# The first layer's second half as seven block products, accumulated by its stores

## The chip, the cores and the metric

The kernel runs on one core of a Trainium2 chip. TensorE (PE) multiplies matrices into the PSUM memory, VectorE (DVE) and ScalarE (ACT) work element by element, GpSimd (POOL) helps out, and SyncE (SP) issues most transfers between the main memory (HBM) and the core's own memory (SBUF). The metric is device time in microseconds (us), the median of several runs. The profile is of one execution. Its times count from the first instruction.

## The reference, cut to what matters

Attention over 4 batches of 8 heads (576 tokens of 64 features, causal, mixed with a memory term by a gate per head) gives `x` of 2304 tokens by 512 features. Two feed-forward layers follow, each 512 to 2048 to 512 features, with different activations:

```python
def _moe_ref(x, w_in, w_out):
    h = x @ w_in
    g = np.where(h >= 1, h, np.where(h <= -1, 0.0, (h + 1) ** 2 / 4))
    return (g @ w_out).astype(np.float32)

def _moe2_ref(x, w_in, w_out):
    h = x @ w_in
    return (np.maximum(0.01 * h, h) @ w_out).astype(np.float32)
```

The layers' weights arrive as 64-bit floating point numbers. The kernel decodes them itself into 32-bit ones.

## The kernel before, in words

**Attention.** `attention_unit` does two heads of one batch, 16 units in all. A list scheduler (`Plan`, with room counts for the buffers, estimated costs and the priorities `PRIO`) writes out one fixed order for every engine before anything runs. Beside the units it schedules `weight_half`, the decoding of the first `EARLY` = 10 halves of weights: a load, two ACT instructions, five DVE instructions (lines 554, 567, 569, 571, 573) and a POOL subtraction (line 558). It also schedules `first_chunk`, which loads the first two token chunks of the layers.

**The layers.** The 2304 tokens are cut into 9 chunks of 256, in groups `(0,1) (2,3) (4,5) (6,7) (8)`: four pairs and a single chunk. There are four segments: layer 0 and layer 1, each in two halves of 1024 hidden features. A half is 8 slots `f` of 128 hidden features. Segment 1 is the second half of layer 0. A step computes the hidden values of one slot for a pair (12 matmuls of 512 columns, lines 798 to 800), or of two slots for the single chunk (24 matmuls of 256 columns). So a segment has 4 x 8 + 4 = 36 steps (`PER`). Every product is made as three matmuls of split operands (`three`: high times high, high times low, low times high), so each hidden value and each weight is needed as a high and a low part. `epilogue` applies the activation (layer 0: ACT lines 855 to 857, then a clamping on DVE, line 859) and makes the two parts (ACT line 865 or 873 the high, DVE line 867 or 875 the low).

**The second product.** About three steps later (`queue` and `pop` in `plan_steps`) PE multiplies those values with the output weights. Segments 0 and 1 do it plainly (`plain`: for each slot of a pair 4 tiles x 3 matmuls of 512 columns). Segments 2 and 3 have `SEVEN` set. There two slots and two column halves form a 2 x 2 block product, which `products` makes of 7 block products instead of 8, 21 matmuls of 256 columns for each chunk and pair of slots. This needs sums of blocks: of the hidden values (`minus` and `sums` in `epilogue`, DVE lines 880 to 885), of the weights (`keep_out` or `split_out`, with extra tiles `ex`), and of the results (`finish`: two ACT copies, line 944, and a third, line 961; DVE lines 948 to 957). The accumulators are the PSUM banks `Ya`, `Yb` and `Y3`. PE takes its tasks strictly by priority (`reach` 1 for PE), and the priority is the step.

**Where results go.** In layer 0 `finish_plain` copies a result into a buffer `lh` (two of them). In segment 0 it is stored to `y_d[0]`. In segment 1 the old sum is loaded into `pp` from `y_d[0]`, added on DVE (line 928) and stored to `y_d[1]`. `load_x` reads that as the input of layer 1. The layout there is features by tokens.

**Weights of later segments.** `weights` schedules, for segments 1 to 3, decoding ahead of time: 12 of 16 halves (`STAGED`: the 8 input halves, then 4 output halves) are decoded from step -29 in distances of 2.0 steps (`DECODE`), written to HBM (`w_d`, `ex_d`) and fetched when their place comes free (`FILL`). The other 4 are decoded directly at the segment's start (`DIRECT`). Transfers wait in order in SP's queue, so a waiting one holds back those behind it.

Of the kernel before, what the change touches and what calls it, by code (L numbers as in the profile page):

```python
# [19 lines left out]
NP = H // 2  # L20
# [8 lines left out]
SEVEN = (False, False, True, True)  # L29
NW, RAWB = 4, 3  # L30

PRIO = dict(load=-650.15, v=946.26, mem=425.05, k=42.8, q=46.21, phi=-70.12, f2=-1390.06, f3=-33.45, f4=-565.0, s0=-357.16,
            s1=-543.91, s2=-387.13, s3=-411.17, t0=49.18, t1=-152.47, t2=-67.16, t3=50.14, v0=-102.73, v1=231.04, v2=1621.08,
            v3=30.63, m=-186.73, d=-177.26, l=-633.13, xm=-415.81, xl=68.91, x=-762.94, b=67.46, w=(4.38, 21.56, 566.24),
            c=291.31)
EARLY, STAY = 10, 167.86
# [97 lines left out]
def attn_moe_moe_kernel(ctx, tc, q, k, v, m_prev, z_prev, beta, w1i, w1o, w2i, w2o, out):  # L134
# [24 lines left out]
    bt = const.tile([128, H], F32, name="bt")  # L159
    gate = const.tile([128, NP, 4], F32, name="gate")  # L160
    gates = const.tile([128, NP, 19], F32, name="gates")
# [15 lines left out]
    pick = const.tile([128, D], F32, name="pick")  # L177
# [57 lines left out]
    y_d = [{g[0]: dram.tile([128, 4, len(g), TC], F32, name=f"y_d{m}_{g[0]}") for g in GROUPS} for m in range(2)]  # L235
# [362 lines left out]
    steps = Plan(dict(x=2, ga=1, gb=1, gg=2, r=1, raw=RAWB - 1, xraw=2, h2=1, w32=NW, da=1, t=1, pp=1, s=1, lh=2, h=1, Ya=1, Yb=1, Y3=1,  # L598
# [16 lines left out]
    PER, AHEAD, DELAY, DIRECT_DELAY = 36, 2, 2, 2  # L615
# [105 lines left out]
    DECODE = [-29 + 2.0 * k for k in range(len(STAGED))]  # L721
    FILL = (-4, -3, -2, -1, -1, 0, 1, 2), (-1, 0, 2, 3)
    DIRECT = {4: 1, 5: 2.2, 6: 3.4, 7: 5}

    def weights(seg):

        base, kept, halves, todo = PER * seg, {}, [], []

        def stage(f, x, prio, after):
            parts = decode(seg, f, x, prio, after)  # L730
            if x == 0 or not SEVEN[seg]:
                kept[f, x] = [keep_half(seg, f, x, *parts, prio)[1]]
                return
            halves.append(parts)
            if f % 2:
                kept[f, x] = kept[f - 1, x] = keep_out(seg, f // 2, *zip(*halves), prio)
                halves.clear()

        def direct(f, prio, after):
            parts = decode(seg, f, 1, prio, after)  # L740
            if not SEVEN[seg]:
                split_half(seg, f, 1, *parts, prio)
                return
            halves.append(parts)
            if f % 2:
                split_out(seg, f // 2, *zip(*halves), prio)
                halves.clear()

        def fetch(room, src, prio, after):
            return steps.add("SP", SEND, prio, after, [room], lambda: nc.sync.dma_start(out=as_r(at(room)), in_=src), lag=6.0)  # L750

        def fill(f, x, prio, after):
            room, after = Room(f"o{f}" if x else f"in{f}"), [*after, *kept[f, x]]
            ready = fetch(room, w_d[seg][f, x], prio, after)
            if x == 0 or not SEVEN[seg]:
                half_room[seg, f, x], half_ready[seg, f, x] = room, ready
                return
            out_room.setdefault((seg, f // 2), []).append(room)
            out_ready.setdefault((seg, f // 2), []).append(ready)
            if f % 2:  # L760
                ex = Room(f"ex{f // 2}")
                out_room[seg, f // 2].append(ex)
                out_ready[seg, f // 2].append(fetch(ex, ex_d[seg][f // 2], prio, after))

        for (f, x), when in zip(STAGED, DECODE):
            todo.append((base + when - AHEAD, lambda after, f=f, x=x, when=when: stage(f, x, base + when + DELAY, after)))
            at_step = FILL[x][f]
            todo.append((base + at_step, lambda after, f=f, x=x, a=at_step: fill(f, x, base + a, after)))
        for f, when in DIRECT.items():
            todo.append((base + when - AHEAD, lambda after, f=f, when=when: direct(f, base + when + DIRECT_DELAY, after)))  # L770
        return todo

    def load_x(seg, group, prio, mm):

        room, ready, n = Room("x"), [], group[0]
        for j, c in enumerate(group):
            raw = Room("xraw")

            def load(c=c, raw=raw):
                xf = staging(at(raw))  # L780
                if SEGS[seg][0] == 0:
                    load_chunk(c, xf)
                else:
                    nc.sync.dma_start(out=xf, in_=y_d[1][n][:, :, c - n])
# [126 lines left out]
    def finish_plain(seg, group, banks, lhs, after, step):  # L911
        half, pair, n, add = SEGS[seg][1], len(group) == 2, group[0], steps.add
        for i, lh in enumerate(lhs):
# [9 lines left out]
            ts = [t]  # L923
            if half:
                pp = Room("pp")
                before = add("SP", SEND, step - 2, [stored_y[seg - 1, n, i]], [pp], lambda pp=pp, place=place: nc.sync.dma_start(
                    out=at(pp).rearrange("p k j t -> p (k j) t"), in_=place(y_d[0])), lag=4.6)
                ts = [add("DVE", dve(512), step, [t, before], [lh, pp], lambda k=k, lh=lh, pp=pp: vec.tensor_tensor(
                    at(lh)[k], at(lh)[k], at(pp)[:, k], ALU.add), lag=SLACK) for k in range(2)]
            t = add("SP", SEND, step + 0.2, ts, [lh], lambda lh=lh, place=place: nc.sync.dma_start(  # L930
                out=place(y_d[half]), in_=at(lh)[2]), lag=4.0)
            stored_y[seg, n, i] = t
            if half:
                for c in group:
                    stored_y.setdefault((seg + 1, c), []).append(t)

    def finish(seg, group, j, banks, y3, lhs, after, step):

        half, pair, c = SEGS[seg][1], len(group) == 2, group[j]
        s, lh, add, tt = Room("s"), lhs[j], steps.add, vec.tensor_tensor  # L940

# [4 lines left out]
        def sums_a():  # L946
            (s0, s1), (lo, hi) = at(s), at(lh)[0:2]
# [6 lines left out]
        def sums_b():  # L954
            (s0, s1), (lo, hi) = at(s), at(lh)[0:2]
            tt(lo[:, 1], s1[:, 0], s1[:, 1], ALU.add)
            tt(lo[:, 0], s1[:, 0], lo[:, 0], ALU.subtract)

        if j == 0:
            for i in range(1 + pair):  # L960
                add("ACT", from_psum(256), step - 2, after, [y3, lhs[i]], lambda i=i: act.activation(
                    at(lhs[i])[0][:, 0], at(y3)[:, i], AF.Copy))
# [3 lines left out]
        ts, goal = [t, t], op_d[c]  # L966
        if half:
            pp, goal = Room("pp"), out[TC * c:TC * c + TC].rearrange("(i p) m -> p i m", i=2)
            before = add("SP", SEND, step - 1, [stored_y[seg - 1, c]], [pp], lambda: load_kept(pp, c), lag=4.0)
            ts = [add("DVE", dve(512), step, [t, before], [lh, pp], lambda i=i: vec.tensor_tensor(  # L970
                at(lh)[i], at(lh)[i], at(pp)[:, i], ALU.add), lag=SLACK) for i in range(2)]
        stored_y[seg, c] = add("SP", SEND, step + 0.2, ts, [lh], lambda: nc.sync.dma_start(
            out=goal, in_=at(lh)[2].rearrange("p (i a) t -> p i (a t)", i=2)), lag=4.0)
# [153 lines left out]
    def take(name, *shape, dt=F32):  # L1127
# [5 lines left out]
                 gg=[[take(f"g{t}{i}", 7, 256, dt=F32R) for t in "hl"] for i in range(2)], r=[take("r", 512)],  # L1133
# [42 lines left out]
```

## Time and profile before

| | us |
|---|---|
| median of 3 runs | 992.94 (992.47 to 993.09) |
| the profiled execution, device time | 992.16 |
| its span from first to last instruction | 990.4 |
| its mean granted TensorE clock | 0.999 of full speed |

The page of the profile gives each engine's busy time and share of the span, then the span in 40 slices, the queues, the chain of work that ended last (followed back from the last instruction), and the costliest groups of instructions. The granted clock is at its upper level, 2.4 GHz, in every slice. A row of a timeline names start, duration, engine, line, operation and output and input. Matmuls overlap, so their durations (0.39 us for 512 columns) are longer than the distance from one start to the next. Attention takes the first 210 us. Then come the segments, with the first steps of segments 1, 2 and 3 at 399, 596 and 787 us.

### The profile page before, as it was taken

The numbers are of one execution on the slowest core, as the hardware profiler recorded it, in microseconds if no ns is written. First come the engines' busy times: TensorE is split into PE (matmuls) and PEld (weight loads), VectorE is DVE, ScalarE is ACT, GpSimd is POOL, SyncE is SP. The second block draws the span as 40 slices with busy tenths as digits, with TensorE's granted clock in tenths as the row PEclk, the third lists the DMA queues.
The fourth block names the chain that finished last, engine by engine and source line by source line (L and its number), as shares of the span: only waits on it lengthen the run. The fifth ranks groups of instructions, "written<-read, shape, count | busy, mean of one in ns | idle before, by whom it ended". The sixth has DMA issues, their size and how long they took to land.

```text
span 990.4 us, 19703 instructions
## 1 busy us (share of the span) xinstructions
PE 975.8 (99%) x7794; PEld 861.4 (87%) x7794; DVE 719.1 (73%) x1569; ACT 597.3 (60%) x1052; POOL 46.4 (5%) x74
## 2 busy tenths in 40 slices
PE   7999999999999999999999999999999999999997
PEld 6888899988888889988888899999999999999997
DVE  7999977759766553486675746997977988755746
ACT  7899888866756465566564654555544554443433
POOL 1332221100000000000000000000000000000000
PEclk9999999999999999999999999999999999999999
DMA  9666743112535442935462669353425790302112
GB/s 199 170 149 152 164 119 98 48 63 90 192 125 173 149 146 80 339 112 157 154 203 70 220 222 355 114 191 133 144 108 181 276 339 13 128 19 89 58 50 85
DMA packets 128556, 145.47 MB, mean 147 GB/s; under 512 B 67792, under 2 KB 103376, under 8 KB 128464
## 3 DMA queue, kind: packets, MB, share of 16 engines
q1 hardware_dynamic: 126976, 143.66, 45.5%
q8 instruction: 61, 1.00, 0.4%
q10 hardware_dynamic: 1488, 0.56, 0.2%
q14 instruction: 31, 0.25, 0.1%
HBM read 98.58 MB, written 45.61 MB: 146 GB/s over the span
## 4 chain that ended last, share of the span: by engine, by line
PE 82%; DVE 9%; ACT 5%; issue 2%; DMA 1%; SPq 0%; DVEq 0%; ACTq 0%
PE h L798 13%; PE h L799 13%; PE h L800 13%; PE Y L799 13%; PE Y L800 13%; PE Y L798 13%; DVE e L403 3%; ACT e L408 3%; PE W L293 2%; DVE ks L348 1%; PE W L438 1%; ACT pt L416 1%; DVE da L567 1%; DVE xm L491 1%; PE W L384 0%
## 5 line engine op out<-in xcount | busy, mean ns | idle before, releaser
L798 PE MATMUL h<-xh,i 128*128 128x512 f32 (+1 forms) x320 | 118.3, 370 | 0.0
L799 PE MATMUL h<-xl,i 128*128 128x512 f32 (+1 forms) x320 | 118.1, 369 | 0.0
L799 PE MATMUL Y<-gl,o 128*128 128x512 f32 (+1 forms) x320 | 117.8, 368 | 0.0
L798 PE MATMUL Y<-gh,o 128*128 128x512 f32 (+1 forms) x320 | 117.7, 368 | 0.0
L800 PE MATMUL h<-xh,i 128*128 128x512 f32 (+1 forms) x320 | 117.7, 368 | 0.0
L800 PE MATMUL Y<-gh,o 128*128 128x512 f32 (+1 forms) x320 | 117.7, 368 | 0.0
L798 PE MATMUL h<-ffn_x,i 128*128 128x512 f32 (+1 forms) x312 | 115.2, 369 | 0.0
L799 PE MATMUL h<-ffn_x,i 128*128 128x512 f32 (+1 forms) x312 | 115.0, 369 | 0.0
L800 PE MATMUL h<-ffn_x,i 128*128 128x512 f32 (+1 forms) x312 | 114.6, 367 | 0.0
L855 ACT ACTIVATE r<-h 128x512 f32<-128x512 f32 x70 | 41.9, 599 | 117.3 <-PE h L800 117.2
L408 ACT ACTIVATE e<-e,mx 128x384 f32<-128x384 f32 (+4 forms) x144 | 71.8, 576 | 16.8 <-DVE mx L403 16.7
L800 PE MATMUL Y<-o,gl 128*128 128x256 f32 x288 | 81.5, 283 | 0.0
L799 PE MATMUL Y<-o,gh 128*128 128x256 f32 x288 | 81.5, 283 | 0.0
L798 PE MATMUL Y<-o,gh 128*128 128x256 f32 x288 | 81.2, 282 | 0.0
L859 DVE SCALAR_TENSOR_TENSOR ga<-ga,r 128x512 f32<-128x512 f32 (+1 forms) x40 | 25.6, 639 | 70.9 <-ACT r L857 70.8
L800 PEld LDWEIGHTS h<-xh,i 128*128 128x128 f32 x320 | 60.3, 189 | 10.3
L865 ACT ACTIVATE gh<-gb 128x512 fp32r<-128x512 f32 (+1 forms) x72 | 53.1, 738 | 26.7 <-DVE gb L885 25.6
L798 PEld LDWEIGHTS Y<-gh,o 128*128 128x128 f32 x320 | 60.3, 189 | 10.1
L800 PEld LDWEIGHTS Y<-gh,o 128*128 128x128 f32 x320 | 60.3, 188 | 10.0
L799 PEld LDWEIGHTS Y<-gl,o 128*128 128x128 f32 x320 | 60.3, 189 | 9.9
L798 PEld LDWEIGHTS h<-xh,i 128*128 128x128 f32 x320 | 60.5, 189 | 9.5 <-ACT gb L852 0.2
L799 PEld LDWEIGHTS h<-xl,i 128*128 128x128 f32 x320 | 60.5, 189 | 8.8
(177 smaller groups left out, 2373.0 us busy)
## 6 DMA issues: line engine op xcount, KB each, us to landing
w_d<-raw SPq DMA_DIRECT2D x36, 512.0 KB, 3.0
raw<-in_moe_w_in_dram SPq DMA_DIRECT2D x32, 512.0 KB, 4.0
raw<-in_moe_w_out_dram SPq DMA_DIRECT2D x32, 512.0 KB, 4.9
i<-w_d SPq DMA_DIRECT2D x24, 512.0 KB, 5.7
y_d<-lh SPq DMA_DIRECT2D x18, 512.0 KB, 4.0
raw<-y_d SPq DMA_DIRECT2D x18, 512.0 KB, 5.9
raw<-x_d SPq DMA_DIRECT2D x12, 512.0 KB, 5.2
o<-w_d SPq DMA_DIRECT2D x12, 512.0 KB, 8.0
```

The lines of the kernel that those rows point to most:

```text
L293: pe.transpose(t[:, c:c + 128], x, ident)
L348: k3 = add("DVE", dve(S), "k", [k2], [t, ks], lambda t=t: vec.tensor_tensor(at(ks)[:, 1], at(t)[:, 0:S], as_r(at(ks)[:, 0]), ALU.subtract))
L403: vec.tensor_tensor_reduce(out=out, in0=src, in1=mk, op0=ALU.add, op1=ALU.min, scale=1.0, scalar=3e38, accum_out=at(st)[1][:, col:col + 1])
L408: lambda x=x, w=w, col=col: act.activation(at(x)[:, 0:w], at(x)[:, 0:w], AF.Exp, bias=at(st)[1][:, col:col + 1], scale=-1.0))
L416: return add("ACT", from_psum(n), key, [t1], [t, room], lambda: act.activation(at(room)[:, 0:n], at(t)[:, 0:n], AF.Copy))
L438: pe.matmul(o[r:r + 64, a:a + W1], at(pt)[:, c + r:c + r + 64], x[:, j, h], start=(j == 0), stop=(j == i))
L798: pe.matmul(o, wh, xh, start=first, stop=False)
L799: pe.matmul(o, wh, xl, start=False, stop=False)
L800: pe.matmul(o, wl, xh, start=False, stop=last)
L855: t1 = add("ACT", from_psum(512), prio, [mm], [hp, r], lambda: act.activation(at(r), at(hp), AF.Relu, bias=0.5, scale=0.5))
L859: new.append(add("DVE", dve(512 if pair else 256), prio, [t, t1], [g[k], r], lambda k=k: vec.scalar_tensor_tensor(out=fresh(k), in0=fresh( ...
L865: h = add("ACT", from_sbuf(width * (b - a)), prio + late, after, [x, gg], lambda: act.activation(view(at(gg)[0])[:, a + c:b + c], view(at( ...
```

## The change

Segment 1 is now a `SEVEN` segment too. Its results come out of `finish`. For the pairs, a POOL transfer adds them onto what segment 0 stored in `y_d` (`accum_op`), so `pp`, the load of the old sum and its addition on DVE go for pairs. The product of the single chunk comes out with tokens on the partitions. `turn_single` turns it with 8 transposes on PE, adds the old sum on DVE and stores it on SP. `y_d` is one array per group instead of two. There are two buffers `r` (half of the activation's square) instead of one. Segment 2's staged decoding has a schedule of its own (`DECODE2`): two halves at steps -64 and -58, so in segment 0, and ten from -30 in distances of 2.3. For segments 1 and 3 the distance is 2.2. The direct decoding of segments 1 and 2 starts 0.5 to 1 step earlier and has a shorter delay (0.5 for 2). Attention decodes 11 halves instead of 10, and all priorities of its plan have other values. Four small tiles move into attention's pool.

```diff
-SEVEN = (False, False, True, True)
+SEVEN = (False, True, True, True)
...
-PRIO = dict(load=-650.15, v=946.26, mem=425.05, k=42.8, q=46.21, phi=-70.12, f2=-1390.06, f3=-33.45, f4=-565.0, s0=-357.16,
...
-            c=291.31)
-EARLY, STAY = 10, 167.86
+PRIO = dict(load=-577.73, v=756.58, mem=328.18, k=39.63, q=46.87, phi=-28.29, f2=-1253.86, f3=-158.15, f4=-1035.0,
...
+            w=(4.77, 24.07, 535.6), c=189.81)
+EARLY, STAY = 11, 157.01
...
-    y_d = [{g[0]: dram.tile([128, 4, len(g), TC], F32, name=f"y_d{m}_{g[0]}") for g in GROUPS} for m in range(2)]
+    y_d = {g[0]: dram.tile([128, 4, len(g), TC], F32, name=f"y_d{g[0]}") for g in GROUPS}
...
-    DECODE = [-29 + 2.0 * k for k in range(len(STAGED))]
+    DECODE = [-30 + 2.2 * k for k in range(len(STAGED))]
+    DECODE2 = [-64 + 6 * k for k in range(2)] + [-30 + 2.3 * k for k in range(10)]
...
-    DIRECT = {4: 1, 5: 2.2, 6: 3.4, 7: 5}
+    DIRECT, DIRECT3 = ({4: 0, 5: 1.5, 6: 3, 7: 4.5}, 0.5), ({4: 1, 5: 2.2, 6: 3.4, 7: 5}, 2)
...
-            if half:
-                pp = Room("pp")
-                before = add("SP", SEND, step - 2, [stored_y[seg - 1, n, i]], [pp], lambda pp=pp, place=place: nc.sync.dma_start(
-                    out=at(pp).rearrange("p k j t -> p (k j) t"), in_=place(y_d[0])), lag=4.6)
-                ts = [add("DVE", dve(512), step, [t, before], [lh, pp], lambda k=k, lh=lh, pp=pp: vec.tensor_tensor(
-                    at(lh)[k], at(lh)[k], at(pp)[:, k], ALU.add), lag=SLACK) for k in range(2)]
...
+        if layer == 0 and not pair:
+            return turn_single(lh, t, banks, step)
+
+        if layer == 0:
+            def add_up():
+                pool.dma_start(out=y_d[n].rearrange("p (b j) i t -> p j b (i t)", j=2)[:, j],
+                               in_=at(lh)[2].rearrange("p (i a) t -> p i (a t)", i=2), accum_op=ALU.add)
+
+            t = add("POOL", 1200, step + 0.2, [t, *(stored_y[0, n, i] for i in range(2))], [lh], add_up, lag=6.0)
+            for x in group:
+                stored_y.setdefault((2, x), []).append(t)
+            return
...
+    def turn_single(lh, t, used, step):
+
+        n, banks, res, pp, add = NCH - 1, Room(used.kind), Room("lh"), Room("pp"), steps.add
+
+        def turn():
+            for i in range(2):
+                x = at(lh)[i].rearrange("p a t -> p (a t)")
+                for et in range(4):
+                    pe.transpose(at(banks)[et // 2][:, et % 2, 128 * i:128 * i + 128], x[:, 128 * et:128 * et + 128], ident)
...
+        before = add("SP", SEND, step - 1, [stored_y[0, n, 0]], [pp], lambda: nc.sync.dma_start(
+            out=at(pp).rearrange("p i a t -> p (i a) t"), in_=whole(y_d)), lag=5.0)
+        t = add("PE", 900, step + 1.2, [t], [lh, banks], turn)
+        ts = [add("DVE", dve(512), step - 1, [t, before], [banks, res, pp], lambda i=i: vec.tensor_tensor(
+            at(res)[i], at(banks)[i], at(pp)[:, i], ALU.add)) for i in range(2)]
+        t = add("SP", SEND, step + 2, ts, [res], lambda: nc.sync.dma_start(out=whole(y_d), in_=at(res)[2]), lag=4.0)
+        stored_y.setdefault((2, n), []).append(t)
...
-                 gg=[[take(f"g{t}{i}", 7, 256, dt=F32R) for t in "hl"] for i in range(2)], r=[take("r", 512)],
+                 gg=[[take(f"g{t}{i}", 7, 256, dt=F32R) for t in "hl"] for i in range(2)], r=[take("r0", 512), take("r1", 512)],
```

## Rows read from the trace of the kernel before

**Rows 1.** The page: busy time of the engines; the last chain by engine.

```profile
PE 975.8 (99%) x7794; PEld 861.4 (87%) x7794; DVE 719.1 (73%) x1569; ACT 597.3 (60%) x1052; POOL 46.4 (5%) x74
...
PE 82%; DVE 9%; ACT 5%; issue 2%; DMA 1%; SPq 0%; DVEq 0%; ACTq 0%
```

**Rows 2.** Timeline of PE (start, us, instruction): first matmuls of groups.

```profile
210.27 0.48 PE L798 MATMUL h<-ffn_x,i 128*128 128x512 f32 x1
...
442.98 0.39 PE L798 MATMUL h<-ffn_x,i 128*128 128x512 f32 x1
...
486.50 0.39 PE L798 MATMUL h<-xh,i 128*128 128x512 f32 x1
...
639.67 0.40 PE L798 MATMUL h<-xh,i 128*128 128x512 f32 x1
...
681.75 0.40 PE L798 MATMUL h<-ffn_x,i 128*128 128x512 f32 x1
```

**Rows 3.** Timeline of DVE in attention, line 355, once a unit ([idle before]).

```profile
46.69 0.75 DVE L355 SCALAR_TENSOR_TENSOR qs<-W,qs 128x576 fp32r<-128x576 f32 x1
...
96.21 0.75 DVE L355 SCALAR_TENSOR_TENSOR qs<-W,qs 128x576 fp32r<-128x576 f32 x1
...
157.66 0.76 DVE L355 SCALAR_TENSOR_TENSOR qs<-W,qs 128x576 fp32r<-128x576 f32 x1 [2.93 <-ACT qs L353]
...
169.61 0.76 DVE L355 SCALAR_TENSOR_TENSOR qs<-W,qs 128x576 fp32r<-128x576 f32 x1 [2.94 <-ACT qs L353]
```

**Rows 4.** Timeline of PE in attention: a run of transposes and what follows.

```profile
164.42 3.08 PE L293 MATMUL W<-ident,e 128*128 128x128 f32 x25
167.33 0.60 PE L342 MATMUL W<-ident,q 128*128 128x128 f32 x4
```

**Rows 5.** Groups of ACT, 640 to 682 us (busy us, mean ns | idle).

```profile
L944 ACT ACTIVATE s<-Y 128x512 f32<-128x512 f32 x4 | 2.2, 597 | 0.0
```

**Rows 6.** Groups of DVE, 640 to 682 us.

```profile
L867 DVE TENSOR_TENSOR gl<-gb,gh 128x512 fp32r<-128x512 f32 (+1 forms) x10 | 8.2, 819 | 0.3 <-ACT gh L865 0.3
...
L957 DVE TENSOR_TENSOR lh<-s,lh 128x256 f32<-128x256 f32 x2 | 0.8, 418 | 0.0
```

**Rows 7.** Windows: length, busy PE, PEld, DVE, ACT, POOL, clock, DMA share, GB/s.

```profile
147.00:159.00 12.00, 11.95 (x221) 10.84 (x218) 8.75 (x32) 10.40 (x19) 1.91 (x4) 1.00 0.47 112
...
443.00:487.00 44.00, 44.00 (x196) 36.44 (x195) 28.81 (x46) 26.57 (x48) 0.00 (x0) 1.00 0.52 168
...
640.00:682.00 42.00, 42.00 (x266) 38.07 (x265) 37.78 (x73) 23.05 (x38) 0.00 (x0) 1.00 0.46 154
...
766.00:787.00 21.00, 21.00 (x177) 20.98 (x176) 19.90 (x45) 11.87 (x27) 0.00 (x0) 1.00 0.66 222
```

**Rows 8.** Groups of DVE, 443 to 487 us: half of the clampings.

```profile
L859 DVE SCALAR_TENSOR_TENSOR gb<-gb,r 128x512 f32<-128x512 f32 x4 | 2.8, 693 | 9.1 <-ACT r L857 9.1
```

**Rows 9.** Groups of DVE, 0 to 209 us: decoding's five instructions.

```profile
L567 DVE SCALAR_TENSOR_TENSOR da<-w,da 128x512 int32<-128x512 int32 x10 | 8.9, 886 | 0.2
...
L573 DVE TENSOR_TENSOR w<-da,dr 128x512 f32<-128x512 f32 x10 | 7.6, 755 | 0.1
L571 DVE SCALAR_TENSOR_TENSOR dr<-raw,dr 128x512 f32<-128x512 uint32 x10 | 6.9, 686 | 0.1
L569 DVE TENSOR_SCALAR dr<-da 128x512 int32<-128x512 int32 x10 | 6.4, 643 | 0.1
...
L554 DVE TENSOR_SCALAR da<-raw 128x512 int32<-128x512 int32 x10 | 4.9, 490 | 0.1
```

**Rows 10.** Transfers of the whole run: KB each, median us to landing.

```profile
y_d<-lh SPq DMA_DIRECT2D x18, 512.0 KB, 4.0
...
pp<-y_d SPq DMA_DIRECT2D x9, 512.0 KB, 4.9
```

**Rows 11.** Timelines of POOL and DVE around 108 us.

```profile
108.06 1.28 POOL L533 TENSOR_TENSOR xr<-xr,xm 128x512 f32<-128x512 f32 x1 [8.69 <-DVE xr L503]
...
108.51 1.38 DVE L567 SCALAR_TENSOR_TENSOR da<-w,da 128x512 int32<-128x512 int32 x1
```

## What I expect, and why

> **What bounds the kernel now.** I read the page's first and fourth parts first: TensorE (PE) is busy for 99% of the span and carries 82% of the chain that ended last, VectorE (DVE) 9% [rows 1]. Busy is modelled for a pipelined engine, so I went on to the waits and the timeline of PE. From 210 us, where the two layers begin, the view of waits names none for PE, and the starts of its matmuls follow each other without a hole, across the ends of chunk groups too: a pair group in the plain form, 192 matmuls of 512 columns, takes 486.50 − 442.98 = 43.52 us [rows 2], 0.2267 us each. So the layers (780 of 990 us) are bound by PE's matmuls, and other work there costs time only where it makes PE wait. The first 210 us, attention, are different. Up to some 120 us DVE starts each instruction as the last ends and a unit takes longer; later DVE sits idle ahead of the same instruction in each unit and PE sets the pace [rows 3].
>
> **The part that the change is about.** A segment has 36 steps: 8 for each of four pairs of chunks and 4 for the single chunk. Segment 1 (the first layer's second half) makes its second product in full, segments 2 and 3 make it of seven block products. Both forms are in the trace, so the gain can be read. A pair takes 43.52 us in the plain form and 681.75 − 639.67 = 42.08 us in the seven form [rows 2]: 1.44 us a pair, 5.76 us for four. (By columns alone it would be an eighth of the product's 21.8 us, 2.7 us; but 42.08 − 96 x 0.2267 = 20.3 us for 168 matmuls of 256 columns is 0.121 us each, and two of them take 0.015 us more than one of 512. That eats almost half.) The single chunk's product has 256 columns in both forms, 8 features x 4 column tiles x 3 = 96 matmuls before and 4 x 7 x 3 = 84 after: 12 x 0.12 = 1.44 us less. Together **−7.20 us** on PE.
>
> **New work on PE.** In the seven form the single chunk's result has tokens on the partitions, while the intermediate array wants features there; `turn_single` adds 8 transposes for it. 25 such transposes took 167.33 − 164.42 = 2.91 us, 0.116 each [rows 4]: **+0.93 us**. They stand in PE's fixed order between two batches of segment 2's first group, and all of segment 2 is queued behind them. They wait for the finish of the single chunk: three ScalarE copies of at most 0.6 us [rows 5], then seven DVE sums of 0.42 [rows 6], 4.7 us. In between PE has the first product of a step (12 x 0.227 = 2.7 us) and a batch of 24 block matmuls (2.9 us), 5.6 us, so they are covered by 0.9 us and the wait is put at 0; with no cover it would be 4.7 us, once. Two DVE additions (0.69 each) must then clear the bank within the next 2.7 us.
>
> **DVE in segment 1** is the cover for all of this, and I cost it from two sides. From the seven side: the second group of segment 2 keeps DVE busy for 37.78 of 42.00 us [rows 7]. The same group in the first layer has 8 clampings of the activation more, 8 x 0.69 = 5.5 [rows 8]; decoding for segment 2 goes from a half every 2.0 steps to one every 2.3, half a weight half less per group, 3.46/2 = 1.7 us [rows 9]. 37.8 + 5.5 − 1.7 = 41.6 us of 42.1. From the plain side: 28.81 us now [rows 7], plus 16 sums of 0.42 (6.7), plus low parts of 8.2 [rows 6] and 4 of 0.69 in place of 8 of 0.69 (5.4), plus the finish, 14 sums of 0.42 in place of 4 additions of 0.69 (3.1), minus 1.7: 42.3, an upper end, since durations of neighbours overlap a little. So DVE is 99 to 101% full. That is tight, but in segment 2's single-chunk window it is busy for 19.90 of 21.00 us while PE misses nothing [rows 7], and PE's second product runs three steps of 5.4 us behind the activations, so that a light group makes up for a full one. The two halves moved to segment 0 and the second `r` buffer lighten it further. Bounds for PE's wait: 0, and (42.3 − 42.1) x 4 = 0.8 us, plus as much at the two ends of the segment. I take **+0.5 us**. In segment 0 the combining and the two halves cost nothing: a plain group leaves DVE idle for 15 of 44 us [rows 7], which covers them; without it each half would cost its 3.5 us.
>
> **The accumulating stores.** Eight stores on GpSimd's queue replace 8 loads of the old sum, 16 DVE additions (counted above) and 8 stores on SP's queue. GpSimd's 46 us of work [rows 1] lie in attention, so nothing is queued behind their wait for the sums. No row shows such a store. The nearest are the plain store and the load that it replaces, 4.0 and 4.9 us to landing [rows 10], 8.9 us together. What waits for it: the `lh` buffer, at the tightest place (last pair to single chunk) four steps of 5.4 us less some 5 us for the sums, so it may take about 16 us; and the next layer's load, over 20 steps later. Cost between 0 and, at twice 8.9 us, 2 us once; I take 0, as 8.9 is nearer. For DVE the nearest row is a GpSimd addition of 1.28 us, beside which a DVE instruction on 512 columns took 1.38 us [rows 11] where 0.69 is usual [rows 8]: 0 to 0.7 us of DVE a store. I take 0, since a store's data don't pass through GpSimd. The Trainium skill, "SBUF — State Buffer", section Who interferes with whom, states that a DVE instruction with two SBUF inputs contends with GpSimd instructions that read SBUF, not with those that only write it; [rows 11] agree with the first half, and no run here shows the second. By that rule an issue that only writes descriptors would cost these sums nothing; one that reads would cost up to 8 x 0.7 = 5.6 us of DVE.
>
> SP's queue loses 16 transfers in segment 1 and gets 6 stores and 2 loads of combined weights; the loads and stores of two halves go to segment 0. No wait of PE in the layers follows a transfer now, and segment 2, which has the same loads, shows none at its start: 0, and if one fill came late, its 5 to 9 us less the steps ahead of it.
>
> **Attention** decodes an eleventh half: five DVE instructions, 0.49 + 0.89 + 0.64 + 0.69 + 0.76 = 3.46 us [rows 9]. Segment 0 then has one less, and no wait to win there. Where DVE is full a unit takes (96.21 − 46.69)/4 = 12.38 us, elsewhere 169.61 − 157.66 = 11.95 [rows 3]. After 120 us the half would cost 0, since DVE is busy only 8.75 of 12 us there [rows 7]; all on the path it costs 3.5. About one half is decoded per unit, so the likeliest is one more full unit: **+0.4 us**. All other priorities of this stage change too. The trace prices that only from both sides: eight full units lose 8 x 0.43 = 3.4 us, which a better order could win back, and I allow as much for a worse one. I take 0 and keep both ends.
>
> **Sum.** The profiled execution took 992.16 us (span 990.4): 992.16 − 7.20 + 0.93 + 0.5 + 0.4 = 986.8. It lies 0.8 below the median of the runs, 992.94, so the forecast for the median is **987.5 us**, 0.55% less; with the small bounds 985.3 to 989.5.
>
> **Rivals.** (a) Attention gains from its new order, 984.1 to 985.3. For it: 3.4 us lie there; against: no row says that the new order finds them. Chance 0.11. (b) Part of the gain is lost to DVE in segment 1 or to waits at its ends: 42.6 to 43.4 us of DVE a group make 0.5 to 1.3 us of wait each, 2 to 5 us: 989.5 to 993. For it: 99 to 101%; against: 95% without a hole in segment 2. 0.13. (c) Attention loses 2 to 5 us, the half wholly on the path and a worse order: 989.5 to 992.5. 0.07. (d) Slower: DVE becomes the bound all through segment 1. Place: its four pair groups, 400 to 575 us. Price: 42.3 us and two stores that each hold DVE for a whole 1.28 us: 44.9, 2.8 over, 11.2 us for four, 998. It decides from 43.5 us a group, where 4 x 1.4 takes back the gain of 5.5; from 44 the kernel is slower. Against it: the issue of a store must hold DVE as long as a computing instruction of GpSimd. 0.07. (e) The seven form gains nothing in the first layer, where the weights stand still and the activations move, the other way about than in segment 2: 994.7. Against it: loads of 128x128 and 256 columns in both. 0.02.
>
> **How the numbers follow.** The forecast (985.3 to 989.5) has 0.60. A measurement of this kernel tells about 0.2%, 2 us, from no change: faster is under 990.95, slower over 994.9. Faster: 0.60, (a), half of (b) and two thirds of (c), 0.82. Same: the rest of (b) and (c), (e), and a little of (d), 0.12. Slower: 0.06. The range takes in the forecast, the near half of (a), and (b) and (c) up to 990.9: 984.7 to 990.9.
>
> **What would show it.** Right: first matmuls of the pair groups of segment 1 42.1 us apart; eight transposes shortly after segment 1 with no hole ahead of them; DVE at 40 to 42 us a group there; segment 2 as now; the first matmul of the layers, now at 210.3 us [rows 2], at 210.7. Wrong: holes in PE's starts in segment 1 that DVE or ScalarE ends (b, d); DVE instructions stretched beside GpSimd's issues (d); accumulating stores that land after more than 16 us and a wait for `lh`; a first matmul that moves by over 2 us (a, c).

## The result, and the profile after

The changed kernel takes 1000.69 us (999.08 to 1001.19, 6 runs) against 992.71 before: 1.0077 times as long, interval 1.0064 to 1.0090. I had forecast 987.5. It is slower by 0.8%, outside my range and on the other side. This is the page of its profile, busy time and the last chain by engine:

```profile
span 999.0 us, 20513 instructions
...
PE 974.7 (98%) x8078; PEld 872.4 (87%) x8078; DVE 787.4 (79%) x1733; ACT 617.0 (62%) x1083; POOL 55.5 (6%) x83
...
PE 76%; DVE 17%; DMA 3%; issue 2%; ACT 1%; SPq 1%; DVEq 0%; ACTq 0%
```

Against [rows 1], PE is busy for no longer, but carries 76% of the chain instead of 82%. DVE has gone from 9 to 17%, and DMA from 1 to 3%. The timeline of PE tells where. These are first matmuls, to be read beside [rows 2]:

```profile
218.47 0.48 PE L800 MATMUL h<-ffn_x,i 128*128 128x512 f32 x1
...
450.63 0.40 PE L800 MATMUL h<-ffn_x,i 128*128 128x512 f32 x1
...
492.71 0.40 PE L800 MATMUL h<-xh,i 128*128 128x512 f32 x1
...
792.02 0.40 PE L800 MATMUL h<-xh,i 128*128 128x512 f32 x1
...
838.41 0.40 PE L800 MATMUL h<-ffn_x,i 128*128 128x512 f32 x1
```

The layers begin at 218.47 instead of 210.27 us: **attention lost 8.2 us**. A pair group of segment 1 takes 492.71 − 450.63 = 42.08 us, exactly the seven form's time. But segment 3's first group, which the change to the product doesn't touch, takes 838.41 − 792.02 = 46.39 us, and 829.98 − 787.42 = 42.56 by these rows of the kernel before:

```profile
787.42 0.50 PE L798 MATMUL h<-xh,i 128*128 128x512 f32 x1
...
829.98 0.40 PE L798 MATMUL h<-ffn_x,i 128*128 128x512 f32 x1
```

From the first matmul to the end of the span the layers take 999.0 − 218.5 = 780.5 us, and 780.1 before: **their gain is used up inside them**. PE's waits from 218 us on, which the kernel before didn't have (us in total, times, longest):

```profile
PE h L800 <- ACT ga L854: 2.1, 1, 2.1
PE Y L997 <- DVE lh L954: 1.2, 1, 1.2
PE h L800 <- ACT gb L858: 1.0, 1, 1.0
PE h L800 <- ACT ga L858: 0.3, 1, 0.3
```

The first is at 808 us, 16 us into segment 3. The matmuls behind it are slow too, so it costs 3.8 us. The others are the wait ahead of the transposes (621 us), the end of segment 1 (599 us) and the end of its last pair (561 us). Together that is some 6.5 us (6.8 by the distances between the matmuls' starts), what was to be gained on balance (7.20 − 0.93 = 6.3).

**Attention.** Line 355 on DVE, once a unit, beside [rows 3]:

```profile
48.74 0.75 DVE L355 SCALAR_TENSOR_TENSOR qs<-W,qs 128x576 fp32r<-128x576 f32 x1
...
100.73 0.75 DVE L355 SCALAR_TENSOR_TENSOR qs<-W,qs 128x576 fp32r<-128x576 f32 x1
...
164.34 0.76 DVE L355 SCALAR_TENSOR_TENSOR qs<-W,qs 128x576 fp32r<-128x576 f32 x1 [2.68 <-ACT qs L353]
...
176.76 0.76 DVE L355 SCALAR_TENSOR_TENSOR qs<-W,qs 128x576 fp32r<-128x576 f32 x1 [2.68 <-ACT qs L353]
```

A unit takes (100.73 − 48.74)/4 = 13.00 us where DVE is full (12.38 before) and 12.42 where it isn't (11.95 before). Both stretches are slower, so two things may be at work. The first shows in the decoding's instructions, 0 to 217 us, beside [rows 9]:

```profile
L567 DVE SCALAR_TENSOR_TENSOR da<-w,da 128x512 int32<-128x512 int32 x11 | 10.7, 976 | 0.3
L573 DVE TENSOR_TENSOR w<-da,dr 128x512 f32<-128x512 f32 x11 | 8.9, 813 | 0.1
...
L569 DVE TENSOR_SCALAR dr<-da 128x512 int32<-128x512 int32 x11 | 8.6, 780 | 0.1
L571 DVE SCALAR_TENSOR_TENSOR dr<-raw,dr 128x512 f32<-128x512 uint32 x11 | 8.2, 749 | 0.1
L554 DVE TENSOR_SCALAR da<-raw 128x512 int32<-128x512 int32 x11 | 6.0, 549 | 0.1
```

The same instructions take longer on average, because more of them take some 0.7 us more. POOL is running whenever one does:

```profile
76.33 1.29 POOL L558 TENSOR_TENSOR o<-w,o 128x512 fp32r<-128x512 f32 x1 [0.18 <-ACT o L562]
...
102.28 1.29 POOL L558 TENSOR_TENSOR o<-w,o 128x512 fp32r<-128x512 f32 x1
```

```profile
76.93 1.24 DVE L567 SCALAR_TENSOR_TENSOR da<-w,da 128x512 int32<-128x512 int32 x1
...
102.72 1.39 DVE L567 SCALAR_TENSOR_TENSOR da<-w,da 128x512 int32<-128x512 int32 x1
```

POOL's instruction ends at 77.62 and at 103.57. The DVE instruction ends 0.55 us after each, so it held still until POOL was nearly done. Summed over the stretched instructions (each one's time over the tenth percentile of its shape) this is 11.5 us after and 6.5 before. Beside line 533, the local sum, it is 6.2 and 5.6. Beside line 558, the decoding's own subtraction, it is 5.3 and 0.9. In the old order POOL's subtraction mostly runs while DVE works on scores out of PSUM (line 403), and none of those is stretched. In the new order the next half's decode instructions stand there.

### The profile page after: what moved, and what is told of

The parts are those of the page before. It is cut to its first block, busy times and chain, and to the rows that moved or that the text cites. A ratio compares the mean times of both kernels' runs of the same rounds, so it can differ in the third digit from the quotient of the medians.

```text
span 999.0 us, 20513 instructions
## 1 busy us (share of the span) xinstructions
PE 974.7 (98%) x8078; PEld 872.4 (87%) x8078; DVE 787.4 (79%) x1733; ACT 617.0 (62%) x1083; POOL 55.5 (6%) x83
## 4 chain that ended last, share of the span: by engine, by line
PE 76%; DVE 17%; DMA 3%; issue 2%; ACT 1%; SPq 1%; DVEq 0%; ACTq 0%
PE h L800 12%; PE h L801 12%; PE h L802 12%; PE Y L802 11%; PE Y L801 11%; PE Y L800 11%; DVE e L403 5%; DMA raw<-in_moe_w_out_dram 2%; PE W L438 2%; DVE xm L491 1%; DVE xr L503 1%; PE W L293 1%; DMA o<-w_d 1%; DVE dr L569 1%; PE W L434 1%
## 5 line engine op out<-in xcount | busy, mean ns | idle before, releaser
L867 ACT ACTIVATE gh<-gb 128x512 fp32r<-128x512 f32 (+1 forms) x108 | 79.8, 739 | 41.7 <-DVE gb L887 33.6
L801 PE MATMUL Y<-gl,o 128*128 128x256 f32 (+1 forms) x288 | 95.1, 330 | 0.0
L802 PE MATMUL Y<-gh,o 128*128 128x256 f32 (+1 forms) x288 | 95.1, 330 | 0.0
L800 PE MATMUL Y<-gh,o 128*128 128x256 f32 (+1 forms) x288 | 94.9, 330 | 0.0
L869 DVE TENSOR_TENSOR gl<-gb,gh 128x512 fp32r<-128x512 f32 (+1 forms) x108 | 88.4, 820 | 7.0 <-ACT gh L867 7.0
L802 PE MATMUL Y<-o,gl 128*128 128x256 f32 x304 | 86.0, 283 | 0.0
L801 PE MATMUL Y<-o,gh 128*128 128x256 f32 x304 | 86.0, 283 | 0.0
L800 PE MATMUL Y<-o,gh 128*128 128x256 f32 x304 | 85.7, 282 | 0.0
L403 DVE CUSTOM_DVE_ANT_0 e<-W,mask 128x384 f32<-128x384 f32 (+4 forms) x144 | 65.8, 510 | 4.9 <-PE W L384 4.8
L800 PEld LDWEIGHTS h<-ffn_x,i 128*128 128x128 f32 x312 | 59.0, 189 | 10.2 <-ACT gb L858 1.2
L802 PEld LDWEIGHTS h<-ffn_x,i 128*128 128x128 f32 x312 | 58.8, 189 | 10.1
```

Of the source, the lines that this page charges most:

```text
L403: vec.tensor_tensor_reduce(out=out, in0=src, in1=mk, op0=ALU.add, op1=ALU.min, scale=1.0, scalar=3e38, accum_out=at(st)[1][:, col:col + 1])
L800: pe.matmul(o, wh, xh, start=first, stop=False)
L801: pe.matmul(o, wh, xl, start=False, stop=False)
L802: pe.matmul(o, wl, xh, start=False, stop=last)
L867: h = add("ACT", from_sbuf(width * (b - a)), prio + late, after, [x, gg], lambda: act.activation(view(at(gg)[0])[:, a + c:b + c], view(at( ...
L869: ready.append(add("DVE", dve(width * (b - a)), prio + late, [h], [x, gg], lambda: tt(view(at(gg)[1])[:, a + c:b + c], view(at(x))[:, a:b] ...
```

## Experiments

The main theory was that attention's 8 us come from its new order, and the rival was the eleventh half or the moved tiles. A second theory explains segment 3's hole by the later decoding schedule, a third the small holes by DVE in segment 1. Times of the runs count against 992.5 to 992.7 for the kernel before, on the same chip as each. In the text "layers at" is the start of the first matmul of the layers; where one row of PE stands alone behind an expectation, it is this matmul. Six of the twelve kernels (old_order_11, new_order_10, new_memset, new_d_xl, old_d_xl, unspread) have one run each; they are read by their traces, since the runs of one kernel differ by 1 to 3 us.

### Which part of attention's change: old_order, old_order_11, new_order_10

```diff
-PRIO = dict(load=-577.73, ... c=189.81)
-EARLY, STAY = 11, 157.01
+PRIO = dict(load=-650.15, ... c=291.31)
+EARLY, STAY = 10, 167.86
```

> The changed kernel with the priorities, STAY and the 10 early halves of the kernel before; all of the layers' change kept. Theory (attention's new order costs its 8.2 us): the layers' first matmul comes back from 218.5 to 210.3 us, the layers keep their 780.5 us, span 990.8, device time 992.5, the same as before. Rival (the four small tiles moved into attention's pool, or anything else outside these lines, slows attention): first matmul later than 214.

```profile
211.25 0.48 PE L800 MATMUL h<-ffn_x,i 128*128 128x512 f32 x1
```

Layers at 211.25, 996.8 us (1.0038, 1.0024 to 1.0051). Seven of the eight microseconds come back, so the order (the priorities and `STAY` together) is the cause. The moved tiles stay moved here, and can account for the last microsecond at most. But the layers now take 784.1 us, 3.5 more than in the changed kernel. 2.7 of them are in segment 1: PE waits 0.9 us on `gb L858` at 411, and 0.6 and 0.2 us on `ga L858` in the pairs where it had waited 0.3 once. Another 1.0 is behind the start of the last group. Ten early halves leave one more to segment 0. The last staged weights for segment 1 go to `w_d` 7.6 us ahead of its start instead of 14.0 (old_order_11, the next run), the raw load behind them goes out 1.5 us after the start instead of 11 us ahead of it, and ACT waits for it with the copies out of `h` in its queue behind. Segment 3 will show the same. This is the wait:

```profile
407.97 0.68 ACT L621 ACTIVATE w<-raw 128x512 f32<-128x512 f32 x1 [3.44 <-DMA raw<-in_moe_w_out_dram]
```

old_order_11 is the same with `EARLY` 11.

> As old_order, but with 11 halves decoded in attention. Theory (the order costs the 8 us, the eleventh half little): first matmul at 210.3 to 211.0 us. Rival (the eleventh half lengthens the stretch in which VectorE is full and costs most of it): 214 or later.

```profile
211.32 0.48 PE L800 MATMUL h<-ffn_x,i 128*128 128x512 f32 x1
```

Layers at 211.32, so the eleventh half costs attention nothing that can be seen, and the hole at segment 1's start is gone: span 991.7, device time 993.47. new_order_10 has the new order and `EARLY` 10.

> The changed kernel with its own priorities, but 10 halves decoded in attention. Theory (order): first matmul between 217 and 218.5 us, and the units that decode nothing still take 12.4 us instead of 11.95. Rival (eleventh half): 213 or earlier.

```profile
218.15 0.48 PE L800 MATMUL h<-ffn_x,i 128*128 128x512 f32 x1
```

Layers at 218.15, 12.43 us a unit in the late stretch, 1002.04 us. The eleventh half isn't the cause; the rival falls.

### What in the order: new_memset, new_d_xl, old_d_xl

```diff
-            pool.tensor_tensor(w[:, 1], got["w"], as_r(w[:, 0]), ALU.subtract)
+            pool.memset(as_r(w[:, 1]), 0.0)
```

> The changed kernel, its own order untouched; only GpSimd's subtraction in the early decoding (the low part of 11 halves) is replaced by filling that low part with zeros, so the low parts of 11 weight halves are left out. Theory (VectorE's decode instructions wait out GpSimd instructions that read the core's memory; in the new order 4 to 5 us of that beside this subtraction): the stretched instructions beside it shrink, and the layers' first matmul comes at 213 to 214.5 us instead of 218.5. Rival (waiting beside GpSimd doesn't matter, the new order's waits of TensorE alone cost the 8 us): 217.5 or later.

```profile
213.86 0.47 PE L800 MATMUL h<-ffn_x,i 128*128 128x512 f32 x1
```

```profile
L558 POOL MEMSET i<- x7: 523/525/528, 19.7 to 136.4; 128x512 f32 x7
L558 POOL MEMSET o<- x4: 524/525/530, 49.8 to 124.9; 128x512 f32 x4
```

The last two rows give the counts, 7 and 4, with shortest, median and longest duration in ns. The kernel leaves out the low parts of these 11 halves. Layers at 213.86: **4.6 us come back** with not one instruction of the order moved, and what DVE waits beside line 558 goes from 5.3 us to nothing. The filling is shorter (0.52 for 1.29 us) and reads nothing, so the run alone doesn't say which of the two did it. One DVE addition that began 0.43 us ahead of a filling's end took its usual time, which speaks for the reading.

new_d_xl sets two priorities of the changed kernel back:

```diff
-d=-31.4, ... xl=-70.9
+d=-177.26, ... xl=68.91
```

> The changed kernel with two of its new priorities set back: d to -177.26 and xl to 68.91, so that the norms of the memory term go ahead of the local rows on VectorE again, as they did. Theory (in the units that decode nothing TensorE's five transposes wait 0.3 us for the memory rows, line 491, which come after the local rows in the new order): those units take 11.95 us instead of 12.4 and the first matmul comes near 215.8. Rival (another priority does it): 12.4 us a unit, first matmul at 218 to 219.

12.1 us a unit in the late stretch instead of 12.42, but layers at 217.91: the decoding stretch, reordered too, ends 1.5 us later and gives most of the gain back. The forecast of 215.8 fell. The counterpart, old_d_xl, has attention's old order with 11 halves and only these two priorities new:

> Attention in the old order with 11 halves (as old_order_11), and only d and xl at their new values (-31.4, -70.9), the counterpart of new_d_xl; segment 3's decoding as in the changed kernel. Theory (these two put the local rows ahead of the memory norms, and five transposes wait for it): units that decode nothing take 12.3 to 12.4 us instead of 11.95, first matmul 213 to 214.5. Rival (they matter only with the rest of the new order): 11.95 us, first matmul 211.3.

```profile
213.80 0.48 PE L800 MATMUL h<-ffn_x,i 128*128 128x512 f32 x1
```

```profile
159.46 0.76 DVE L355 SCALAR_TENSOR_TENSOR qs<-W,qs 128x576 fp32r<-128x576 f32 x1 [2.68 <-ACT qs L353]
...
171.79 0.76 DVE L355 SCALAR_TENSOR_TENSOR qs<-W,qs 128x576 fp32r<-128x576 f32 x1 [2.68 <-ACT qs L353]
```

12.33 us a unit, layers at 213.80, and 211.32 in old_order_11: **2.5 us from two numbers**. In the new order the local rows (lines 503 and 497) go ahead of the memory norms (467, 471) on DVE, so the memory rows (491) come later, and their PSUM bank is the one that PE's next five transposes need. In the changed kernel that wait shows as

```profile
174.14 0.77 PE L293 MATMUL W<-ident,e 128*128 128x128 f32 x5 [0.32 <-DVE xm L491]
```

The same wait of 0.32 us is in old_d_xl; in old_order_11 and new_d_xl the five transposes follow without one.

4.6 + 2.5 = 7.1 of the 8.2 us. That these two add up is not shown. The first was taken off the changed kernel and the second put onto the old order; taken off the changed kernel, the second alone gave back 0.6, and no run has both. The rest is open: the eight kernels here with the old order, old_d_xl left out, begin their layers at 210.5 to 211.8, and I have one profile of the kernel before, at 210.3.

### Segment 3's start: old_order_decode3

```diff
+    DECODE3 = [-29 + 2.0 * k for k in range(len(STAGED))]
...
-        for (f, x), when in zip(STAGED, DECODE2 if seg == 2 else DECODE):
+        for (f, x), when in zip(STAGED, {1: DECODE, 2: DECODE2, 3: DECODE3}[seg]):
```

> As old_order, and segment 3 has the old schedule of staged decoding back (from step -29 in distances of 2.0; segment 1 keeps 2.2, segment 2 its own). Theory (the hole of 2.2 us at segment 3's start, and the 12 matmuls at the lower clock behind it, come from the last staged weights reaching SP's queue about 14 us later, so that the next raw load is late and holds ScalarE's queue): the hole goes, segment 3's first group takes 42.3 instead of 46.4 us, span 986.8, device time 988.5. Rival (the transfers at that boundary are late for another reason, the full DMA engines): the hole stays above 1.5 us and the time at 992.

```profile
787.20 0.50 PE L801 MATMUL h<-xh,i 128*128 128x512 f32 x1
...
829.79 0.40 PE L801 MATMUL h<-ffn_x,i 128*128 128x512 f32 x1
```

Segment 3's first group takes 42.59 us instead of 46.57 in old_order, and the hole is gone: the later schedule is the cause. The time is 992.83 us, 4.0 below old_order (the forecast of 988.5 lacked the holes that 10 halves bring to segment 1). What happened in the changed kernel stands in ACT's timeline:

```profile
802.24 0.85 ACT L867 ACTIVATE gh<-gb 128x768 fp32r<-128x768 f32 x1 [0.74 <-DVE gb L887]
808.87 0.67 ACT L621 ACTIVATE w<-raw 128x512 f32<-128x512 f32 x1 [5.78 <-DMA raw<-in_moe_w_out_dram]
809.44 0.58 ACT L854 ACTIVATE ga<-h 128x512 f32<-128x512 f32 x1
```

Line 854 empties the one bank `h` that PE needs for its next step. It stands in ACT's queue behind line 621, which waits 5.8 us for a raw load. The load is the first of these two rows, 7.4 us into the segment; before, the second, it went out 3.1 us ahead. It also takes 9.4 us to land instead of 6.4:

```profile
799.41 0.33 SPq L250 DMA_DIRECT2D raw<-in_moe_w_out_dram  x1
```

```profile
784.34 0.42 SPq L250 DMA_DIRECT2D raw<-in_moe_w_out_dram  x1
```

In SP's queue it stands behind the stores of the last staged weights. The last of them to `w_d` are this row after, and the second before:

```profile
789.79 0.92 SPq L649 DMA_DIRECT2D w_d<-raw  x2
```

```profile
775.37 0.92 SPq L649 DMA_DIRECT2D w_d<-raw  x2
```

That is 2.2 us ahead of the segment's start instead of 12.

### The three together: best1, and two tries at the rest: best2, best3

best1 has the old priorities, 11 halves and segment 3's old schedule.

> The changed kernel with the old priorities and STAY, 11 early halves, and segment 3's old decode schedule: the three findings so far together. Theory: first matmul of the layers at 211.3 us, no hole in segment 1's first three groups, segment 3's first group 42.6 us, span 987.7, device time 989.5, 0.3% below the kernel before. Rival (the holes are tied to each other and come back elsewhere): 992 or more.

990.21 us, 0.9972 (0.9962 to 0.9983): **0.28% faster than the kernel before**, about half of what I had forecast for the change (987.5, 0.55%). Its remaining waits in the layers:

```profile
PE h L801 <- ACT gb L859: 1.0, 1, 1.0
PE Y L998 <- DVE lh L955: 0.8, 1, 0.8
...
PE h L801 <- ACT ga L859: 0.3, 1, 0.3
```

best2 also gives segment 2's direct decoding its old, later start (`DIRECT3 if seg >= 2`).

> As best1, and the direct decoding for segment 2 starts as late as before the change (steps 1, 2.2, 3.4, 5 with delay 2 instead of 0, 1.5, 3, 4.5 with 0.5). Theory (the two holes at the ends of the single chunk, 1.1 us ahead of segment 2 and 0.8 us ahead of the transposes, come from VectorE and ScalarE having direct decoding among the single chunk's work): both holes shrink below 0.4 us, span 986.0 to 986.4, device time 988. Rival (the decoding is then late for the products of features 4 to 7): a hole of 1 us or more some steps into segment 2, span 987.7 or more.

990.78 us. The wait at 592 us halves (0.5) and another of 0.4 comes up at 784; that ahead of the transposes stays at 0.7. The expectation fell: segment 2's direct decoding makes half of the first and little of the second. best3 moves a third half into segment 0.

```diff
-    DECODE2 = [-64 + 6 * k for k in range(2)] + [-30 + 2.3 * k for k in range(10)]
+    DECODE2 = [-64 + 6 * k for k in range(3)] + [-30 + 2.3 * k for k in range(9)]
```

> As best1, but three instead of two of segment 2's halves are decoded in segment 0, so the last one of segment 1 is done 2.3 steps earlier. Theory (the holes of 0.4 us ahead of the single chunk and 1.1 us ahead of segment 2 come from VectorE being full in the last pair and the single chunk, with ScalarE's copies out of the bank h queued behind): both shrink to below 0.6 us together, segment 0 keeps its 188.6 us, span 987.0 to 987.6 against best1's 988.3. Rival (these holes come from the order within the single chunk's own work): span stays at 988.0 to 988.6.

992.91 us, layers 779.5 instead of 776.8. The last pair has DVE busy for less (38.36 of 43.00 us instead of 40.39) and keeps its hole; new waits of 1.1, 0.3 and 0.5 us open in segment 1's first groups. The theory fell, and the span, 990.6 us, lies outside the rival's range too. A few per cent of DVE's time decide little here; that it matters more which instruction stands ahead of ACT's copy out of `h` is a reading of the traces.

### The change's own means: accum_sp, unspread

accum_sp is best1 with the pairs' results added by a load, two DVE additions and a store instead of the accumulating store:

```diff
-            t = add("POOL", 1200, step + 0.2, [t, *(stored_y[0, n, i] for i in range(2))], [lh], add_up, lag=6.0)
+            pp = Room("pp")
+            before = add("SP", SEND, step - 2, [stored_y[0, n, i] for i in range(2)], [pp], lambda: nc.sync.dma_start(
+                out=at(pp).rearrange("p i a t -> p i (a t)"), in_=whole(y_d)), lag=4.6)
+            ts = [add("DVE", dve(512), step, [t, before], [lh, pp], lambda k=k: vec.tensor_tensor(
+                at(lh)[k], at(lh)[k], at(pp)[:, k], ALU.add), lag=SLACK) for k in range(2)]
+            t = add("SP", SEND, step + 0.2, ts, [lh], lambda: nc.sync.dma_start(
+                out=whole(y_d), in_=at(lh)[2].rearrange("p (i a) t -> p i (a t)", i=2)), lag=4.0)
```

> As best1, but the pairs' results of segment 1 are added the old way: a load of the old sum on SP, two additions on VectorE, a store on SP, instead of GpSimd's accumulating store. Theory (the accumulating stores take 1.2 us a chunk off VectorE at no cost, where it has 2 to 4 us to spare a group): VectorE goes to 41 to 42 us a group and holes of 1 to 4 us in sum come up in segment 1, span 989 to 992. Rival (the stores bring nothing, VectorE had room): 988.0 to 988.6.

996.11 us, 5.9 more than best1, almost all of it in the last pair and the single chunk (47.11 and 23.32 us instead of 42.67 and 22.36). PE waits 3.4 us once for a copy out of `h`, in a stretch in which DVE has no pause and ACT waits for DVE:

```profile
PE h L801 <- ACT ga L859: 3.4, 1, 3.4
```

So the stores are worth more than I thought, in one place rather than in every group. unspread is best1 with segment 2's staged decoding all in segment 1 (`DECODE2 = [-29 + 2.0 * k for k in range(12)]`).

> As best1, but segment 2's staged decoding has the schedule that it had before the change: all 12 halves within segment 1, every 2.0 steps from step -29. Theory (VectorE's demand, not its share alone, decides: some 40 us a group become 41.5 to 43): holes of 2 to 6 us in sum in segment 1's pairs, its span over 195 us instead of 192.7. Rival (the three steps that TensorE runs behind take it up): no new hole, 192.7.

Span 994.1, 5.8 more than best1. The holes sit in the single chunk (26.56 instead of 22.36 us) and behind it, not in the pairs. DVE has no pause there from 580 to 597 us, so the backlog of twelve halves seems to pile up and come out at the end. The size was as expected, the place not.

## Why the prediction was wrong, point by point

The profiled execution took 1000.8 us, 14.0 more than the 986.8 of my sum. 7.8 of them are in attention (8.2 for my 0.4) and 6.3 are PE's waits in the layers (6.8 for my 0.5).

**The product.** Right: 42.08 us for the second and the third pair, as in segment 2. Without the 6.8 us of holes the layers take 773.8 us, 6.3 less than before, and 7.20 − 0.93 = 6.3. The 7.2 us were there.

**Attention: the step that failed.** I wrote that the new priorities are priced only from both sides, took 0 and kept ±3.4. Set back, they return 7.2 of the 8.2 us. The bound itself was wrong: I made it of what eight DVE-full units lose to the PE-paced ones, which says what an order can win back, and used the same figure for a loss. A loss has no such floor. Two rows that I had quoted carry it. [rows 11] show a decode instruction waiting for POOL, at 0.7 us a time, which I weighed only against the accumulating stores; the new order makes that wait happen more often (4.6 us by new_memset, where the filling is both shorter and reads nothing). And [rows 7], at 11.95 us of PE in 12.00, leave nothing to spare in the late units: any instruction that comes later there costs its delay in each unit (2.5 us by old_d_xl). The eleventh half, which I did price (0.4), cost 0.1 us in the old order and 0.3 in the new.

**Segment 3: a part that I left out.** The diff moves the staged decoding of segments 1 and 3 from "−29 + 2.0 k" to "−30 + 2.2 k", so the last half is 1.2 steps later. I looked at DVE for segments 1 and 2 and wrote that SP's moves cost 0 because no PE wait follows a transfer. SP's queue at segment 3 had no line of mine, and my bound for a late fill was for weights that PE waits for, not for a raw load that ACT waits for. It cost 3.8 us in the changed kernel, by way of a late raw load and ACT's order.

**DVE in segment 1.** Too high in demand, too low in effect. The windows after, beside [rows 7]:

```profile
451.00:493.00 42.00, 42.00 (x266) 38.07 (x265) 38.45 (x75) 29.39 (x52) 2.31 (x2) 1.00 0.49 138
493.00:535.00 42.00, 42.00 (x265) 38.10 (x264) 36.15 (x69) 27.94 (x50) 2.16 (x2) 1.00 0.44 113
535.00:577.00 42.00, 41.73 (x261) 37.61 (x260) 39.29 (x78) 28.66 (x53) 2.15 (x2) 1.00 0.44 119
```

DVE is busy 38.5, 36.2 and 39.3 us of 42, not 41.6 to 42.3: I had left the direct halves' lows (2.3 us, lines 712 and 716) in the window that I started from. PE still waits, 1.3 us at the segment's last two boundaries where I had 0.5 for all, since a share over 42 us says nothing of the 10 us (589 to 599) in which two loads' low parts, the last pair's finish and the single chunk's sums stand in DVE's queue without a pause, and ACT waits for them with the copy out of `h` behind.

**The transposes.** 0.8 us where I had read 0.93; but the cover of 0.9 us that I worked out was none:

```profile
622.60 1.06 PE L997 MATMUL Y<-ident,lh 128*128 128x128 f32 x8 [1.17 <-DVE lh L954]
```

I counted the finish's three copies and seven sums as if they started at once. The single chunk's last product ends at 615.6 us, but the copies start at 617.30, since this instruction stands ahead of them in ACT's queue:

```profile
616.20 0.68 ACT L621 ACTIVATE w<-raw 128x512 f32<-128x512 f32 x1 [2.26 <-DMA raw<-in_moe_w_out_dram]
```

And DVE puts three sums of the next step's activations between the finish's fifth and sixth. In best2, where the copies start at once, DVE has decode work ahead of the sums and PE still waits 0.7 us.

**The accumulating stores.** Right. They land in 6.9 us, in between the bounds of 0 and 16, and 30 DVE instructions that run beside their issue are stretched by 0.007 us at most:

```profile
y_d<-lh POOLq DMA_DIRECT2D x8, 512.0 KB, 6.9
```

**Segment 0's half.** I wrote that there was no wait to win there. In old_order, with that half in segment 0, segment 1 loses 2.6 us against old_order_11: the wait to win was one segment on.

**Rivals.** (c) had the right place and, in its worse order, half of the right mechanism, at a price of 2 to 5 us and a chance of 0.07; its other half, the eleventh half on the path, cost next to nothing. The waits at segment 1's ends (b) and segment 3's came on top. The chance of 0.82 for faster came from adding parts that could be read and setting those that couldn't to zero.

## What to carry to other kernels

A change that rewrites a fixed order is not neutral by default: where one engine has 0.05 us of 12 to spare, list which instruction comes later for whom, and price a loss by what can come to wait (here instructions of DVE that meet POOL's), not by what could be won. Go through every schedule line of a diff segment by segment, those of segments that keep their computation too. Where PE works through a single bank, look at what stands ahead of the copy that empties it in its engine's fixed order; that queue is in the chain of nearly every hole seen here, the one ahead of the transposes included; an engine's share of a whole group doesn't say where they come.

## What I had not expected of the hardware

A DVE instruction that starts while a POOL instruction is reading the same memory takes until 0.13 us before POOL's end and then its own time: 17 cases after and 10 before, each 0.55 to 0.72 us longer but one, for instructions with two inputs from SBUF (lines 567, 571, 573, 589) and for those with one (554, 569). Those that read PSUM (403, 348, 491) were not stretched, and neither was line 471, a reciprocal of ten numbers a partition in SBUF, in six such cases; why stays open. That agrees with the Trainium skill, "SBUF — State Buffer", section Who interferes with whom, for two inputs against a reading GpSimd; and of the issue of an accumulating store, 1.08 us on POOL, the trace shows no such effect on DVE.

A hole of 2.3 us in PE's work (at 808 us in the changed kernel; lengths here are what the distance between two starts has over its usual one) was followed by a granted clock of 0.76 over this stretch:

```profile
807.00:814.00 7.00, 4.89 (x19) 3.87 (x18) 4.76 (x10) 3.61 (x7) 0.00 (x0) 0.76 1.06 389
```

Matmuls of 512 columns were 0.427 instead of 0.227 us apart for some 3 us, which is the lower of the two levels (1.2 of 2.4 GHz), and so the hole cost 3.8 us, 1.7 times its length. It was the same in old_order, old_order_11, new_order_10, new_d_xl and old_d_xl at this place, behind the hole of 3.5 us in accum_sp, and behind one of 2.0 us in unspread (0.76 from 586 to 593 us). In new_memset a hole of 2.3 us at this place had no such end (1.00 from 802 to 809 us), nor had the 2.3 us between two other matmuls with the transposes in them at 621 us. What tells them apart stays open.
